# One layer of linear attention with a gated unit: the first tiles' work in another order, operand addresses at multiples of 512 bytes, query steps in smaller pieces

## The chip, the cores and the metric

The kernel runs on one core of one Trainium2 chip. A core has five instruction queues that run beside each other and meet only at semaphores: TensorE (PE in the profile, with PEld for its loads of weights), VectorE (DVE), ScalarE (ACT), GpSimd (POOL) and SyncE (SP), which here issues DMAs alone. Each queue executes its instructions in the order in which they stand in the program. The metric is the device time of one execution in microseconds, lower is better; with several runs the median counts.

## The reference, cut to what matters

The input x has 2048 rows of 512. All of it is float32.

```python
xn = _layernorm(x)
# _A_ref(xn): 32 heads of 16
q, k, v = xn @ wqkv
pq = q @ w_phi;  pk = k @ w_phi                  # per head
phi_q = concat(softmax(pq), softmax(-pq))        # 32 features a head
phi_k = concat(softmax(pk), softmax(-pk))
kv = phi_k^T v;  z = sum over rows of phi_k
s = ((phi_q @ kv) / (phi_q @ z + 1e-6)) @ wo
# _B_ref(xn): 1376 features
g = silu((relu(xn @ W_gate) * (xn @ W_up)) @ W_down)
return x + s * g
```

## The kernel before, in words

**Tiles.** The 2048 rows are 16 tiles of 128. The list `order` takes them in pairs of two blocks, so that tiles 0 and 1, 2 and 3 and so on of the list (this text counts by the list) belong to two blocks that are worked on together. Products run in float32r: each operand is split into a hi part (a copy rounded by ScalarE) and a lo part (the rest, by VectorE or GpSimd), and `mm3` makes three matmuls of one product: lo by hi, hi by lo, hi by hi. Weights for the keys and queries are first multiplied by `w_phi` (`fold`), so that a projection gives pk and pq directly.

**First stage: keys and values.** For each tile n the loop at the end of `layer_kernel` does this: load x; layer norm; transpose on TensorE (`turn`, tile `pxT`), whose result ScalarE copies as the hi part into `XT` and once more as `xf`, and VectorE completes with the lo part (`lo_xt`); project to pk and pv (12 matmuls of 512 columns each); `features`, which turns pk into phi on VectorE and ScalarE (largest and smallest of each head into `mx`, two subtractions into `ek`, two Exp, sum `sm`, reciprocal, product) and splits v into `vhl`; `query`, the projection of an earlier tile to pq, stored to DRAM; `features_split`, which splits phi into hi and lo (`phl`, the lo part on GpSimd) and adds phi to `zacc` with an accumulating DMA; and `kv_products` of tile n-2, which adds phi^T v into four PSUM banks that stay taken (`pkv`). For each odd tile, GpSimd makes four sums and differences of the two tiles of a pair (`sums_x`, tiles `sa` and `sb`), whose hi and lo parts (`sums_hi`, `sums_lo`) also go into `XT`; the second stage uses them.

**Norms.** There are two ways to do a layer norm. `norm_stats`, `norm_scale`, `norm_apply` let ScalarE sum and square and apply (each with a little VectorE, and a power of -0.5 on GpSimd with the constant `mhalf`). `norm_vector` and `norm_vector_apply` do it on VectorE (statistics, aggregate, add, then one two-scalar operation), with the same power on GpSimd. Before the change tiles 0 to 3 go by the second way, all others by the first.

**Before the loop.** The loads of x and of three weights are issued on SyncE; weights arrive while tile 0 is normed. Then, written out by hand: fold and split of the key weights (`wkh`, `wkl`), norm and transpose of tiles 0 and 1, pk of tile 0, hi and lo parts of the value weights (`wv_hi` on ScalarE, `wv_lo` on GpSimd), fold and split of the query weights (`wqh`, `wql`), norms of tiles 2 to 5.

**Second stage: the gated unit.** Eleven blocks of 128 features, in two halves of the rows. `gate_up` computes gate and up for two blocks of rows at once by a scheme of seven products (`pa`, `pb`, `pc`, `pd`) on sums of the operands, of which VectorE reads each result before the next may be added into the same PSUM bank; `down` multiplies with W_down (`py`). Beside it run, in small steps: the preparation of the weights (`f_prep`, sums and splits on GpSimd and ScalarE, stored to DRAM for the second half), and the queries (`q_pair`: fetch and transpose of pq, `bounds`, `shift`, Exp, sums, division, and `q_back`, which multiplies with kv, tile `pnum`). At the end of each half `out_tile` multiplies with wo (`pso`) and combines.

**What sets the order.** All instructions of a queue stay in the order in which the program issues them. A small planner (`Clock`, called `pace`) decides at building time where steps written as generators are put: it keeps an estimate of when each engine is free and each tile ready, and `pump` issues the next step of each generator when its engine's estimated backlog is below a limit. For the preparation of weights that limit is two times the value in `LIMIT` (2,500 ns for GpSimd). A step is what lies between two `yield`s.

**Memory.** Tiles come from pools: `u8`, `u4` and `u2` are slots of 8, 4 and 2 KB a partition; PSUM has eight banks, used in turn (`ps`), so that a new tile waits until the one eight places earlier has been read. In the built program the constants of the compiler take 128 bytes a partition ahead of the first tile. `XT` and all `u8` and `u2` slots start at 128 modulo 512, and the `u4` slots, which come after `ident` (512 bytes) and `mhalf` (128 bytes), at 256 modulo 512. In the matmuls the tiles of value features (`vhl`), of the attention output (`oh`, `ol`) and of transposed phi (`pTh`, `pTl`) come from `u4`; all others come from `XT`, `u8` and `u2`.

Of the kernel before, what the change touches and what calls it, by code (L numbers as in the profile page):

```python
# [13 lines left out]
P = 128  # L14
# [134 lines left out]
def layer_kernel(ctx: ExitStack, tc: tile.TileContext, x, wkT, wqT, wv, wo, wf, cst, out):  # L149
# [12 lines left out]
    def u4(shape, name, dt=F32):  # L162
        return sb.tile(list(shape), dt, tag="u4", bufs=B4, name=name)
# [4 lines left out]
    def small(n, name, bufs=3):  # L168
        return sb.tile([P, n], F32, tag=name, bufs=bufs, name=name)
# [71 lines left out]
        return lambda: split(*map(by_parity, w[k]), even_first(p))  # L241


    XT = sb.tile([P, 8, 2, 2, BT], F32R, tag="XT", name="XT")
    pace.shared = XT.name
    XN, XF, SF = {}, {}, {}
# [128 lines left out]
                PQ[q] = dram((P, 2, 2 * P), f"pq{q[0]}{q[1]}")  # L375
            pace.when(t, lambda q=q, col=col, part=part: nc.sync.dma_start(PQ[q][:, col, :], t[:, part, :]))

    def features(n, pk, pv, between):

        vhl = u4((P, NG, 2, 64), "vhl", F32R)  # L380
        pvg = pv.rearrange("p (g f) -> p g f", g=NG)
        pkv_ = pk.rearrange("p (h f) -> p h f", f=DH)
        sm = small(64, "sm", 2)
        e = u4((P, H, 2, DH), "ek")
        mx = sb.tile([P, 2, H], F32, tag="mx", bufs=2, name="mx")
        nc.vector.tensor_reduce(mx[:, 0, :], pkv_, op=ALU.max, axis=AX.X)
        nc.vector.tensor_reduce(mx[:, 1, :], pkv_, op=ALU.min, axis=AX.X)
        for s in range(2):
            top = mx[:, s, :].unsqueeze(2).to_broadcast([P, H, DH])
            a, b = (top, pkv_) if s else (pkv_, top)  # L390
            nc.vector.tensor_tensor(e[:, :, s, :], a, b, op=ALU.subtract)
            nc.scalar.activation(e[:, :, s, :], e[:, :, s, :], AF.Exp)
            if s == 0:
                nc.scalar.activation(vhl[:, :, 0, :], pvg, AF.Copy)
        between()
        add(nc.vector, vhl[:, :, 1, :], pvg, f32(vhl[:, :, 0, :]), ALU.subtract)
        nc.vector.tensor_reduce(sm, groups(e), op=ALU.add, axis=AX.X)
        nc.vector.reciprocal(pv[:, 0:64], sm)
        VH[n] = vhl
        phi = e if n else zacc  # L400
        nc.vector.tensor_tensor(groups(phi), groups(e), pv[:, 0:64].unsqueeze(2).to_broadcast([P, 64, DH]), op=ALU.mult)
        EK[n] = phi
# [228 lines left out]
    def q_pair(q):  # L631
# [10 lines left out]
        def bounds(j):  # L642
            mx.append(sb.tile([P, 2, H], F32, tag="mx", bufs=2, name="mx"))
            nc.vector.tensor_reduce(mx[j][:, 0, :], pv[j], op=ALU.max, axis=AX.X)
            nc.vector.tensor_reduce(mx[j][:, 1, :], pv[j], op=ALU.min, axis=AX.X)
# [27 lines left out]
        fetch(0)  # L673
        yield "vector", pv[0]
        bounds(0)
        shift(0)
        yield "scalar", es[0]
        expo(0)
# [1 line left out]
        fetch(1)  # L680
        yield "vector", pv[1]
        bounds(1)
        shift(1)
        if q + 1 < NP:
            q_load(q + 1)
# [209 lines left out]
    p = ps((P, P), name="pidle")  # L895
    for _ in range(14):
        nc.tensor.matmul(p, idle, idle, start=True, stop=True)
    mhalf = sb.tile([P, 32], F32, name="mhalf")[:, 0:1]
    nc.vector.memset(mhalf, -0.5)
    zacc = u4((P, H, 2, DH), "zacc")  # L900

# [18 lines left out]
    norm_vector_apply(1)  # L920
    pk = project(0, WK, "pk")
    folds = [fold(WQ, wq_raw[:, k, :], k) for k in range(2)]
    for k in range(KD):
        wv_hi(k)
        if k < 3:
            wv_lo(k)
    folds[0]()
    norm_vector(2)
    folds[1]()
    full_xt(*px)  # L930
    px = turn(1)
    norm_vector_apply(2)
    folds = [fold(WQ, wq_raw[:, k, :], k) for k in range(2, KD)]
    lo_xt(*px)
    wv_lo(3)
    norm_vector(3)
    folds[0]()
    norm_vector_apply(3)
    folds[1]()
    norm_stats(4)  # L940
    norm_scale(4)
    norm_stats(5)

    def all_preps():
        for f in AHEAD:
# [14 lines left out]
    for n in range(N):  # L960
        at[0] = n
        if n + 7 < N:
            load_x(n + 7)
        if n == 2:
            preps = pace.add(all_preps(), 0, 2)
        if n + 4 < N:
            norm_apply(n + 4)
        if n + 5 < N:
            norm_scale(n + 5)
        if n:  # L970
            pk = project(n, WK, "pk")
        if n == 1:
            third = turn(LEAD)
            sums_x(LEAD)
        turned = turn(n + LEAD) if 0 < n < N - LEAD else None
        pace.pump()
        if turned and turned[0] % 2 and n:
            sums_x(turned[0])
        pv = project(n, WV, "pv")
        if n == 0:  # L980
            turned = turn(2)
        pace.pump()

        def between():
            if n == 1:
                lo_xt(*third)
            if turned:
                lo_xt(*turned)
        features(n, pk, pv, between)
        if n >= 1:  # L990
            query(n - 1)
            pace.pump()
            if n % 2 == 0 and n - 1 < N // 2:
                pace.later(4, lambda n=n: spill_x(n - 1))
        if n == 0:
            sums_x(1)
            sums_hi(1)
            sums_lo(1)
        if n + 6 < N:
            norm_stats(n + 6)  # L1000
        if n % 2 and n + 2 < N:
            sums_hi(n + 2)
        features_split(n)
        if n % 2 and n + 2 < N:
            sums_lo(n + 2)
        if n >= 2:
            kv_products(n - 2)
            pace.pump()
# [214 lines left out]
```

## Time and profile before

| | us |
|---|---|
| median of 3 runs | 573.58 (572.75 to 573.88) |
| the profiled execution | 574.12 |
| its span | 572.3 |
| TensorE busy | 563.2 |
| VectorE busy | 411.4 |
| ScalarE busy | 281.4 |
| GpSimd busy | 413.9 |

The profile is of one execution. Its page gives for each engine the time in which it had an instruction running. [...] Rows in order of time give start, duration, engine, line, operation, output and inputs; line 52 is a helper that issues every operation, so tiles tell the operations apart. A matmul of float32 operands has two records, one of float32r has one. The granted clock was 1.00 throughout.

### The profile page before, as it was taken

The numbers are of one execution on the slowest core, as the hardware profiler recorded it, in microseconds if no ns is written. First come the engines' busy times: TensorE is split into PE (matmuls) and PEld (weight loads), VectorE is DVE, ScalarE is ACT, GpSimd is POOL, SyncE is SP. The second block draws the span as 40 slices with busy tenths as digits, with TensorE's granted clock in tenths as the row PEclk, the third lists the DMA queues.
The fourth block names the chain that finished last, engine by engine and source line by source line (L and its number), as shares of the span: only waits on it lengthen the run. The fifth ranks groups of instructions, "written<-read, shape, count | busy, mean of one in ns | idle before, by whom it ended". The sixth has DMA issues, their size and how long they took to land.

```text
span 572.3 us, 8310 instructions
## 1 busy us (share of the span) xinstructions
PE 563.2 (98%) x2688; PEld 470.4 (82%) x2688; DVE 411.4 (72%) x613; ACT 281.4 (49%) x503; POOL 413.9 (72%) x351
## 2 busy tenths in 40 slices
PE   8899999999999999999999999999999999999997
PEld 8787888888888788888888888888888888888886
DVE  4799677676755899699797442599896969874322
ACT  3699687775535436435435142223545544534510
POOL 1569988899867267989986434554669888888476
PEclk9999999999999999999999999999999999999999
DMA  8348999956598918788787999996656766569783
GB/s 292 117 147 216 255 261 276 262 168 184 156 264 261 378 63 293 269 295 273 243 291 254 223 362 417 395 356 243 180 189 208 233 204 195 170 203 312 186 223 144
DMA packets 84682, 138.24 MB, mean 242 GB/s; under 512 B 7840, under 2 KB 34336, under 8 KB 83744
## 3 DMA queue, kind: packets, MB, share of 16 engines
q1 hardware_dynamic: 81184, 125.60, 64.6%
q0 software_dynamic: 3312, 12.06, 11.2%
q8 instruction: 21, 0.34, 0.2%
q14 instruction: 21, 0.17, 0.1%
q10 hardware_dynamic: 144, 0.07, 0.0%
HBM read 77.14 MB, written 52.69 MB: 227 GB/s over the span
## 4 chain that ended last, share of the span: by engine, by line
PE 88%; DVE 5%; POOL 2%; DMA 2%; ACT 1%; issue 1%; SPq 1%; POOLq 0%; DVEq 0%
PE py L52 20%; PE pa L52 10%; PE pc L52 10%; PE pd L52 10%; PE pso L52 8%; PE pq L52 7%; PE pk L52 6%; PE pv L52 6%; PE pb L52 5%; PE pnum L52 3%; PE pkv L52 3%; DMA wvr<-wv 2%; SPq L52 1%; DVE mx L52 1%; PE pxT L52 1%
## 5 line engine op out<-in xcount | busy, mean ns | idle before, releaser
L52 PE MATMUL py<-fdh,hl 128*128 128x512 f32 x176 | 68.5, 389 | 0.0
L52 PE MATMUL py<-fdh,hh 128*128 128x512 f32 x176 | 68.5, 389 | 0.0
L52 PE MATMUL py<-fdl,hh 128*128 128x512 f32 x176 | 68.5, 389 | 0.0
L52 PE MATMUL pa<-XT,wa 128*128 128x512 f32 x264 | 67.6, 390 | 0.0
L52 POOL TENSOR_TENSOR hl<-e,hh 128x512 fp32r<-128x512 f32 x22 | 28.7, 1305 | 42.4 <-ACT hh L52 37.8
L52 PEld LDWEIGHTS pa<-XT,wa 128*128 128x128 f32 x264 | 49.3, 188 | 10.3
L52 ACT ACTIVATE hh<-e 128x512 fp32r<-128x512 f32 x22 | 13.9, 633 | 74.9 <-DVE e L52 65.4
L52 POOL TENSOR_TENSOR phl<-ek,phl 128x1024 fp32r<-128x1024 f32 x15 | 36.1, 2405 | 17.1 <-ACT phl L52 17.1
L52 DVE TENSOR_TENSOR y<-py,y 128x512 f32<-128x512 f32 x40 | 27.5, 688 | 26.8 <-PE py L52 26.6
L52 POOL TENSOR_TENSOR hl<-u,hh 128x512 fp32r<-128x512 f32 x22 | 28.9, 1312 | 23.0 <-ACT hh L52 22.9
L52 PE MATMUL pv<-wvh,XT 128*128 128x512 f32 x128 | 43.5, 401 | 0.0
L52 PE MATMUL pk<-wkh,XT 128*128 128x512 f32 x128 | 42.5, 393 | 0.9 <-DVE ek L52 0.9
L52 PE MATMUL pq<-XT,wqh 128*128 128x512 f32 (+1 forms) x144 | 40.4, 366 | 0.0
L52 PEld LDWEIGHTS py<-fdh,hh 128*128 128x128 f32 x176 | 33.0, 188 | 6.9
L52 PEld LDWEIGHTS py<-fdh,hl 128*128 128x128 f32 x176 | 33.0, 188 | 6.8
L52 PEld LDWEIGHTS py<-fdl,hh 128*128 128x128 f32 x176 | 33.0, 188 | 6.8
L52 POOL TENSOR_TENSOR ez<-eq,zB 128x1024 f32<-128x1024 f32 x16 | 38.5, 2418 | 0.0
L52 PE MATMUL pc<-XT,wc 128*128 128x512 f32 x132 | 35.3, 395 | 0.8 <-DVE e L52 0.8
L52 POOL TENSOR_TENSOR ol<-of,oh 128x1024 fp32r<-128x1024 f32 x8 | 19.2, 2408 | 23.1 <-ACT oh L52 11.2
L52 PE MATMUL pd<-XT,wd 128*128 128x512 f32 x132 | 34.2, 393 | 0.0
L52 PE MATMUL pd<-XT,wc 128*128 128x512 f32 x132 | 33.8, 389 | 0.0
L52 PE MATMUL pc<-XT,wb 128*128 128x512 f32 x132 | 33.7, 389 | 0.0
(154 smaller groups left out, 1598.2 us busy)
## 6 DMA issues: line engine op xcount, KB each, us to landing
zacc<-ek POOLq DMA_DIRECT2D x15, 512.0 KB, 5.4
xts<-XT SPq DMA_DIRECT2D x4, 1792.0 KB, 11.8
XT<-xts SPq DMA_DIRECT2D x7, 1024.0 KB, 17.6
wa<-ws SPq DMA_DIRECT2D x26, 256.0 KB, 3.8
wb<-ws SPq DMA_DIRECT2D x26, 256.0 KB, 5.3
wc<-ws SPq DMA_DIRECT2D x26, 256.0 KB, 5.3
rawg<-wf SPq DMA_DIRECT2D x22, 256.0 KB, 4.4
ws<-wa SPq DMA_DIRECT2D x22, 256.0 KB, 5.6
```

What stands on the lines that cost most here:

```text
L52: return self.tc.keep_in_program_order(op(*a, **k))
```

## The change

- **Addresses.** `mhalf` is made first and with 96 floats instead of 32, so 384 bytes lie between the compiler's 128 and `XT`. `XT` and all `u8`, `u4` and `u2` slots then start at multiples of 512 bytes.
- **`features` in three functions.** `exponents` (maxima, minima and subtractions on VectorE), `exp_part` (one Exp on ScalarE) and the rest. For tile 0, `exponents` is issued right after its pk and the first four parts of the value weights, and both Exp before the loop; for the other tiles the order is as it was.
- **Value weights.** Each lo part follows its hi part; parts 0 and 1 come before the splits of the first two query weights, 2 and 3 after them. All four lo parts are issued before the norms of tiles 2 and 3.
- **Norms.** Tile 4 is normed on VectorE, tile 5 on ScalarE; in the loop, the apply of tile 4 stands at n = 0 and that of tile 5 at n = 1.
- **Sums of tile 1.** `sums_x(1)` and `sums_hi(1)` are issued before the loop, `sums_lo(1)` at n = 1.
- **Transposes.** At n = 0, pk of tile 1 comes before the transpose of tile 2. At n = 1, tile 3 is transposed before pv of tile 1 and tile 4 after it; before, both came ahead of pv.
- **Split of tile 0's phi.** `features_split(0)` moves from the end of n = 0 into n = 1, ahead of the features of tile 1.
- **Preparation of weights.** Its limit goes from two to three.
- **Query steps.** In `q_pair` a `yield` stands between `bounds` and `shift`, for both halves, so that the planner may issue other work between them.

```diff
@@ -241,6 +241,7 @@
         return lambda: split(*map(by_parity, w[k]), even_first(p))
 
 
+    mhalf = sb.tile([P, 96], F32, name="mhalf")[:, 0:1]
     XT = sb.tile([P, 8, 2, 2, BT], F32R, tag="XT", name="XT")
     pace.shared = XT.name
     XN, XF, SF = {}, {}, {}
@@ -375,12 +376,9 @@
                 PQ[q] = dram((P, 2, 2 * P), f"pq{q[0]}{q[1]}")
             pace.when(t, lambda q=q, col=col, part=part: nc.sync.dma_start(PQ[q][:, col, :], t[:, part, :]))
 
-    def features(n, pk, pv, between):
-
-        vhl = u4((P, NG, 2, 64), "vhl", F32R)
-        pvg = pv.rearrange("p (g f) -> p g f", g=NG)
+    def exponents(pk):
+
         pkv_ = pk.rearrange("p (h f) -> p h f", f=DH)
-        sm = small(64, "sm", 2)
         e = u4((P, H, 2, DH), "ek")
         mx = sb.tile([P, 2, H], F32, tag="mx", bufs=2, name="mx")
         nc.vector.tensor_reduce(mx[:, 0, :], pkv_, op=ALU.max, axis=AX.X)
@@ -389,9 +387,21 @@
             top = mx[:, s, :].unsqueeze(2).to_broadcast([P, H, DH])
             a, b = (top, pkv_) if s else (pkv_, top)
             nc.vector.tensor_tensor(e[:, :, s, :], a, b, op=ALU.subtract)
-            nc.scalar.activation(e[:, :, s, :], e[:, :, s, :], AF.Exp)
-            if s == 0:
-                nc.scalar.activation(vhl[:, :, 0, :], pvg, AF.Copy)
+        return e
+
+    def exp_part(e, s):
+        nc.scalar.activation(e[:, :, s, :], e[:, :, s, :], AF.Exp)
+
+    def features(n, e, raised, pv, between):
+
+        vhl = u4((P, NG, 2, 64), "vhl", F32R)
+        pvg = pv.rearrange("p (g f) -> p g f", g=NG)
+        sm = small(64, "sm", 2)
+        if not raised:
+            exp_part(e, 0)
+        nc.scalar.activation(vhl[:, :, 0, :], pvg, AF.Copy)
+        if not raised:
+            exp_part(e, 1)
         between()
         add(nc.vector, vhl[:, :, 1, :], pvg, f32(vhl[:, :, 0, :]), ALU.subtract)
         nc.vector.tensor_reduce(sm, groups(e), op=ALU.add, axis=AX.X)
@@ -673,6 +683,7 @@
         fetch(0)
         yield "vector", pv[0]
         bounds(0)
+        yield "vector", pv[0]
         shift(0)
         yield "scalar", es[0]
         expo(0)
@@ -680,6 +691,7 @@
         fetch(1)
         yield "vector", pv[1]
         bounds(1)
+        yield "vector", pv[1]
         shift(1)
         if q + 1 < NP:
             q_load(q + 1)
@@ -895,7 +907,6 @@
     p = ps((P, P), name="pidle")
     for _ in range(14):
         nc.tensor.matmul(p, idle, idle, start=True, stop=True)
-    mhalf = sb.tile([P, 32], F32, name="mhalf")[:, 0:1]
     nc.vector.memset(mhalf, -0.5)
     zacc = u4((P, H, 2, DH), "zacc")
 
@@ -920,26 +931,31 @@
     norm_vector_apply(1)
     pk = project(0, WK, "pk")
     folds = [fold(WQ, wq_raw[:, k, :], k) for k in range(2)]
-    for k in range(KD):
+    for k in range(2):
         wv_hi(k)
-        if k < 3:
-            wv_lo(k)
+        wv_lo(k)
+    early = exponents(pk)
     folds[0]()
+    folds[1]()
+    for k in range(2, KD):
+        wv_hi(k)
+        wv_lo(k)
     norm_vector(2)
-    folds[1]()
     full_xt(*px)
     px = turn(1)
+    lo_xt(*px)
+    folds = [fold(WQ, wq_raw[:, k, :], k) for k in range(2, KD)]
+    for s in range(2):
+        exp_part(early, s)
+    norm_vector(3)
     norm_vector_apply(2)
-    folds = [fold(WQ, wq_raw[:, k, :], k) for k in range(2, KD)]
-    lo_xt(*px)
-    wv_lo(3)
-    norm_vector(3)
+    sums_x(1)
     folds[0]()
+    folds[1]()
     norm_vector_apply(3)
-    folds[1]()
-    norm_stats(4)
-    norm_scale(4)
     norm_stats(5)
+    norm_vector(4)
+    sums_hi(1)
 
     def all_preps():
         for f in AHEAD:
@@ -962,45 +978,49 @@
         if n + 7 < N:
             load_x(n + 7)
         if n == 2:
-            preps = pace.add(all_preps(), 0, 2)
-        if n + 4 < N:
+            preps = pace.add(all_preps(), 0, 3)
+        if n == 0:
+            norm_vector_apply(4)
+        elif n + 4 < N and n > 1:
             norm_apply(n + 4)
         if n + 5 < N:
             norm_scale(n + 5)
-        if n:
+
+        now, late = {0: ((), ()), 1: ((3,), (4,))}.get(n, ((n + LEAD,) if n < N - LEAD else (), ()))
+        if n > 1:
             pk = project(n, WK, "pk")
-        if n == 1:
-            third = turn(LEAD)
-            sums_x(LEAD)
-        turned = turn(n + LEAD) if 0 < n < N - LEAD else None
+        turned = [turn(m) for m in now]
         pace.pump()
-        if turned and turned[0] % 2 and n:
-            sums_x(turned[0])
+        for m in now:
+            if m % 2:
+                sums_x(m)
         pv = project(n, WV, "pv")
         if n == 0:
-            turned = turn(2)
+            pk = project(1, WK, "pk")
+            turned = [turn(2)]
+        turned += [turn(m) for m in late]
+        if n == 1:
+            norm_apply(5)
+            features_split(0)
+            sums_lo(1)
         pace.pump()
 
         def between():
-            if n == 1:
-                lo_xt(*third)
-            if turned:
-                lo_xt(*turned)
-        features(n, pk, pv, between)
+            for t in turned:
+                lo_xt(*t)
+        e, early = early or exponents(pk), None
+        features(n, e, n == 0, pv, between)
         if n >= 1:
             query(n - 1)
             pace.pump()
             if n % 2 == 0 and n - 1 < N // 2:
                 pace.later(4, lambda n=n: spill_x(n - 1))
-        if n == 0:
-            sums_x(1)
-            sums_hi(1)
-            sums_lo(1)
         if n + 6 < N:
             norm_stats(n + 6)
         if n % 2 and n + 2 < N:
             sums_hi(n + 2)
-        features_split(n)
+        if n:
+            features_split(n)
         if n % 2 and n + 2 < N:
             sums_lo(n + 2)
         if n >= 2:
```

## The prediction

> **What bounds the kernel now.** I read the page's first lines, then the list of what TensorE waited for, then the rows in order of time around each wait.
>
> ```profile
> span 572.3 us, 8310 instructions
> PE 563.2 (98%) x2688; PEld 470.4 (82%) x2688; DVE 411.4 (72%) x613; ACT 281.4 (49%) x503; POOL 413.9 (72%) x351
> PE 88%; DVE 5%; POOL 2%; DMA 2%; ACT 1%; issue 1%; SPq 1%; POOLq 0%; DVEq 0%
> ```
>
> TensorE is busy for 563.2 of 572.3 us and holds 88% of the chain. The change takes no matrix product away, so time can come from only two places: the 9.1 us in which PE is idle, and the spacing of the 2688 matmul records. The profiled execution took 574.12 us, 1.8 us more than its span; the runs' median is 573.58, 0.54 below it. I work out differences on the trace and take them from 573.58.
>
> ```profile
> PE pxT L52 <- ACT xn L52: 1.2, 1, 1.2
> PE pk L52 <- DVE ek L52: 0.9, 1, 0.9
> PE pv L52 <- POOL wvl L52: 0.8, 1, 0.8
> PE pc L52 <- DVE e L52: 0.8, 1, 0.8
> ```
>
> Four waits of 3.7 us in all (columns: sum, times, longest). The first three lie in the first 44 us, where the change reorders work; the fourth is in the query steps, which the change cuts up. So each part of the edit does face a wait. But a wait that goes may only uncover the next one, so I walk through both places.
>
> **The head, up to the third tile.** Rows of the trace in order of time (start, duration, engine, output<-inputs; in brackets the idle time before):
>
> ```profile
> 13.54 1.51 DVE L52 TENSOR_SCALAR xn<-xt,bm,br 128x512 f32<-128x512 f32 x1
> 15.96 1.15 ACT L52 ACTIVATE wvh<-wvr 128x512 fp32r<-128x512 f32 x2 [2.26 <-DMA wvr<-wv]
> 17.63 0.69 DVE L52 TENSOR_TENSOR wql<-pfold,wqh 128x512 fp32r<-128x512 f32 x1 [2.58 <-ACT wqh L52]
> 18.02 0.48 PE L52 MATMUL pv<-wvh,XT 128*128 128x512 f32 x1
> 19.99 1.29 POOL L52 TENSOR_TENSOR wvl<-wvr,wvh 128x512 fp32r<-128x512 f32 x1
> 21.34 0.50 PE L52 MATMUL pv<-wvl,XT 128*128 128x512 f32 x1 [0.78 <-POOL wvl L52]
> 22.08 0.68 DVE L52 BATCH_NORM_STATS2 bs<-xt 128x6 f32<-128x512 f32 x1
> 23.90 0.55 DVE L52 TENSOR_SCALAR xn<-xt,bm,br 128x512 f32<-128x512 f32 x1
> 25.10 0.60 PE L52 MATMUL pxT<-ident,xn 128*128 128x128 f32 x4
> 25.96 1.28 DVE L52 TENSOR_REDUCE mx<-pk 128x32 f32<-128x512 f32 x2
> 26.89 0.65 PE L52 MATMUL pxT<-ident,xn 128*128 128x128 f32 x4 [1.19 <-ACT xn L52]
> 27.16 0.68 DVE L52 TENSOR_TENSOR ek<-pk,mx 128x512 f32<-128x512 f32 x1
> 28.86 0.74 POOL L52 TENSOR_TENSOR sb<-xf,sa 128x256 f32<-128x256 f32 x1
> 29.02 0.69 DVE L52 TENSOR_TENSOR vhl<-pv,vhl 128x512 fp32r<-128x512 f32 x1
> 43.03 0.68 DVE L52 TENSOR_TENSOR ek<-mx,pk 128x512 f32<-128x512 f32 x1
> 43.86 0.47 PE L52 MATMUL pk<-wkh,XT 128*128 128x512 f32 x1 [0.92 <-DVE ek L52]
> 50.75 0.68 DVE L52 TENSOR_TENSOR ek<-mx,pk 128x512 f32<-128x512 f32 x1
> 53.56 0.39 PE L52 MATMUL pk<-wkh,XT 128*128 128x512 f32 x1
> ```
>
> *Parts of the weights.* Now the last lo part of wv waits on POOL behind a norm's pow and ends at 21.28, 0.06 before PE resumes. The change issues all four lo parts before that norm. Their hi parts need the DMA, which lets ScalarE start at 15.96. ScalarE now first does the two wqh parts (before, they came after wvh), so wvh 2 and 3 end at about 17.65 instead of 17.1. POOL then does two lo parts of 1.29 each from 17.15 and ends at about 19.75. PE begins pv at 18.02 and comes to the last lo part, its eleventh matmul, some 2.4 us later (0.3 for the first, then 0.23 each), at 20.4. The wait of 0.8 goes, with 0.1 of restart.
>
> *Exponents of tile 0.* Two reductions and two subtractions (25.96 to 28.4: about 2.4 us) move to 15.05, where DVE sat idle for 2.58 us. Their cover is that idle time. They end at 17.5, and wql starts where it did. The two Exp of tile 0 also go to an earlier place on ScalarE; nothing of PE waits there.
>
> *Norms.* Tile 4's norm moves from ScalarE (two passes, accumulators, an apply) to DVE: statistics (0.68 at 22.08 for tile 3), two small operations and an apply (0.55 at 23.90). The apply is dear when POOL is working: the row at 13.54 has the same operation at 1.51. [...] That price is at stake for tile 3, because the sums of tile 1 (four POOL pieces of about 0.74, here the last is at 28.86) now run at about 22.0 to 24.9. So tile 3's apply ends between 24.0 and 25.4. Its transpose is wanted at about 23.95 (pv until 20.75, pk's twelve matmuls until 23.5, then tile 2's transpose) and waits 0.2 to 1.5 us instead of the 1.2 for tile 4 now. Tile 4's transpose comes after a whole pv and doesn't wait.
>
> *What is late next.* Those two gains are not simply the answer, for the next wait is DVE's. The third tile's pk takes a PSUM bank that is free only after the subtractions of tile 2 (43.03 + 0.68). From vhl at 29.02 to the end of these DVE is busy but for about 1.0 us. In the new order vhl's turn comes at about 27.75. Its hi part on ScalarE now stands behind the hi copies of the sums (new place), which wait for the last POOL piece at 24.9; then come two copies of a tile's transpose and vhl itself, 0.5 each, up to 27.0; then DVE does tile 2's lo part. From there the same 14.7 us of work, less up to 1.0 of idle time, ends at 41.5 to 42.5. PE itself would be there at 40.9 plus the small wait above. So pk starts at 41.6 to 42.6 instead of 43.86: 1.3 to 2.3 us off. I take 1.8, the middle. All three head waits together are worth that and not the 2.9 they add up to. One tile later DVE's subtraction ends at 51.43 and PE comes at 53.56: 2.1 us in hand, so nothing is given back there.
>
> *More preps.* Limit 2 becomes 3, so weights for the gate stage enter the queues of POOL and ScalarE sooner and stand ahead of the split of phl. A phl is used two tiles later:
>
> ```profile
> 42.31 2.38 POOL L52 TENSOR_TENSOR phl<-ek,phl 128x1024 fp32r<-128x1024 f32 x1 [2.59 <-ACT phl L52]
> 52.60 1.13 PE L52 MATMUL pkv<-phl,vhl 128*128 128x256 f32 x8
> ```
>
> It ends at 44.7 and is wanted at 52.6, so 7.9 us cover what is put before it (a 128x512 POOL piece is 1.29). Its price is nothing; without that cover two pieces, 2.6 us. SP's stores of prepared weights and loads of x move with it; no PE row waits for them here, and I cost them at nothing.
>
> **The query steps.** A yield between bounds and shift lets other DVE work in.
>
> ```profile
> 186.21 1.29 DVE L52 TENSOR_REDUCE mx<-pq 128x32 f32<-128x512 f32 x2
> 188.01 0.68 DVE L52 TENSOR_TENSOR eq<-mx,pq 128x512 f32<-128x512 f32 x1
> 189.60 1.52 PE L52 MATMUL pd<-XT,wc 128*128 128x512 f32 x6
> 190.53 0.72 DVE L52 STREAM_TRANSPOSE pq<-pql 128x512 f32<-128x512 f32 x1
> 191.15 0.67 DVE L52 TENSOR_TENSOR e<-pc,u 128x512 f32<-128x512 f32 x1
> 191.88 1.67 PE L52 MATMUL pc<-XT,wc 128*128 128x512 f32 x6 [0.76 <-DVE e L52]
> ```
>
> PE adds to pc only after DVE has read it. It would come there at 190.96 (six matmuls from 189.60) and starts at 191.88. In the new program the first reduction is followed by two of the gate stage's DVE operations instead of the subtractions, and the read of pc stands before the second transpose, not behind it: it ends 0.6 to 0.7 sooner, at 191.2. Of 0.92 about 0.25 is left: 0.7 off, with 0 (another operation takes the place) and 0.9 as bounds. The later query steps hold up no PE row now and cost nothing: the same instructions in another order beside a busy PE.
>
> **The addresses.** mhalf's tile of 384 bytes before XT, instead of 128 behind the identity, moves XT, the 8 KB and 2 KB tiles from 128 to 0 modulo 512 and the 4 KB tiles from 256 to 0. It adds no instruction. What it may do is seen where the two operands of a matmul now differ:
>
> ```profile
> 30.49 0.28 PE L52 MATMUL pq<-XT,wql 128*128 128x256 f32 x1
> 32.65 0.28 PE L52 MATMUL pq<-XT,wql 128*128 128x256 f32 x1
> 200.74 0.39 PE L52 MATMUL py<-fdl,hh 128*128 128x512 f32 x1
> 201.65 0.39 PE L52 MATMUL py<-fdh,hh 128*128 128x512 f32 x1
> 545.13 0.40 PE L52 MATMUL pso<-woh,ol 128*128 128x512 f32 x1
> 547.92 0.39 PE L52 MATMUL pso<-woh,ol 128*128 128x512 f32 x1
> ```
>
> py has weights and moving rows both at 128: its two rows are four matmuls apart, 227 ns each. pso has its weights in 4 KB tiles (256) and its moving rows at 128: twelve apart, 232 ns each. If the addresses cause that, all pairs at 0 agree as py's do, and pso's 180 matmuls of 512 columns gain 5 ns: 0.9 us. No row has a pair at 0, so the bounds come from both sides. The two pq rows are 18 matmuls of 256 columns apart, 120 ns each; 256 columns more cost 107 ns, so 512 alone are 214 and 13 ns are a floor under every matmul. At best that floor goes (13 ns better), at worst all pairs do as pso does (5 ns worse). I take py's value, since every pair that now agrees modulo 512 has it.
>
> Sum: 1.8 + 0.7 + 0.9 = 3.4 off 573.58, forecast **570.2 us** (0.6%).
>
> **Rivals.**
> *(a) The floor falls.* The 13 ns come from operands that straddle 512-byte blocks, and go: 2512 matmuls (2184 of 512 columns, 328 of 256) by 13 ns are 32.7 us, with the 2.5 of the reordering about 538. For it: the floor is the same at both sizes, as if it came with the 512 bytes of weights. Against: nothing shows that addresses cause it. [...]
>
> *(b) The other side: residue 0 doesn't settle.* Then the 2004 other matmuls of 512 columns are spaced as pso's are, 5 ns more: 10.0, against 2.5 off: 581.1. It decides from 1.3 ns per matmul on. For it: pso shows that an address alone may cost this much. Against: there the operands differ, here they agree.
>
> *(c) POOL holds PE up.* Tile 3's apply is blocked more than once, or preps push phl past its 7.9 us, and the planner's new order repeats it at a later tile: two pieces of 1.29 at each of two places, 5.2, less 3.4: 575.4. For it: the apply at 13.54. Against: phl's slack.
>
> *(d) It doesn't do what it says.* DVE's chain holds pk at 43.8 as now, e still comes late, pso stays at 232: 573.6.
>
> **How the numbers follow.** Forecast 0.57, (a) 0.11, (b) 0.09, (c) 0.12, (d) 0.11. A change under 0.2% (1.15 us) can't be told from none. Faster: the forecast and (a), 0.68; same: (d), 0.11; slower: (b) and (c), 0.21. The likeliest case's own range is 568.7 (the waits wholly gone, 2.9 + 0.9 and restarts of 0.2, and pso's 0.9) to 572.3 (the head's lower bound alone). The range of 8 in 10 takes in (c) and (d) and, below, a floor that falls by a quarter, 3 ns on 2184 matmuls, 6.6 more off: 563.5 to 575.5. It leaves out (b) and the full (a).
>
> **What would show it.** Right: the last wv lo ends near 19.8 and pv runs through; the third tile's pk starts near 42; the waits for xn, wvl and e in the list of waits are under 0.3 or gone; pso's rows 227 ns apart. Wrong: py's rows more than 1 ns off 227 (addresses decide all); pk at 43.8 (DVE's chain was not shortened); a new wait of PE for phl.

## The result, and the profile after

The changed kernel takes 569.81 us (median of 20 runs, 567.54 to 575.55), the kernel before on the same chip 573.75 (20 runs, 572.75 to 574.99). The ratio is 0.9937, with a 95% interval of 0.9917 to 0.9957: 0.6% faster. 570.2 was forecast. The spread is new: the kernel before stays within 2.3 us, the changed one covers 8, and four of its 20 runs lie above 573.

The profiled execution of the changed kernel happens to be the longest of all, 575.55 us. Two lines of its page (the busy times, and the share of each engine in the chain that ended last):

```profile
PE 562.5 (98%) x2688; PEld 472.0 (82%) x2688; DVE 410.3 (72%) x615; ACT 280.3 (49%) x498; POOL 413.3 (72%) x351
PE 82%; DMA 6%; DVE 4%; issue 3%; POOL 3%; ACT 1%; SPq 0%; POOLq 0%; ACTq 0%; DVEq 0%
```

DMA has risen from 2% to 6% of the chain. What TensorE waited for in it (sum, times, longest), in a span of 573.7 us:

```profile
PE pv L52 <- ACT pqs L52: 3.2, 1, 3.2
...
PE pk L52 <- DVE ek L52: 0.8, 1, 0.8
PE pso L52 <- POOL ol L52: 0.4, 1, 0.4
```

The waits for xn, wvl and e of the profile before are gone. A wait of 3.2 us that was not there stands at the head of the list. The same kernel was profiled a second time, in an execution of 570.48 us, 5.1 shorter, with a span of 568.7 us:

```profile
PE pk L52 <- DVE ek L52: 1.6, 2, 0.8
...
PE pso L52 <- POOL ol L52: 0.4, 1, 0.4
```

Here the wait of pv for pqs is missing, though DMA still has 4% of this chain, so the rise by itself is not that wait. This is the execution to compare with the profile before. Its first 42 us, in order of time (start, duration, engine, output and inputs, idle time before):

```profile
16.66 0.67 DVE L52 TENSOR_TENSOR ek<-mx,pk 128x512 f32<-128x512 f32 x1
17.17 2.55 POOL L52 TENSOR_TENSOR wvl<-wvr,wvh 128x512 fp32r<-128x512 f32 x2 [1.09 <-ACT wvh L52]
17.26 1.27 DVE L52 TENSOR_TENSOR wql<-pfold,wqh 128x512 fp32r<-128x512 f32 x2
17.92 0.48 PE L52 MATMUL pv<-wvh,XT 128*128 128x512 f32 x1
22.74 0.99 DVE L52 TENSOR_SCALAR xn<-xt,bm,br 128x512 f32<-128x512 f32 x1
23.48 1.03 PE L52 MATMUL pxT<-ident,xn 128*128 128x128 f32 x8
27.41 0.68 DVE L52 TENSOR_TENSOR vhl<-pv,vhl 128x512 fp32r<-128x512 f32 x1
40.32 0.68 DVE L52 TENSOR_TENSOR ek<-mx,pk 128x512 f32<-128x512 f32 x1
41.14 0.47 PE L52 MATMUL pk<-wkh,XT 128*128 128x512 f32 x1 [0.79 <-DVE ek L52]
```

PE begins pv 0.1 us earlier than before (17.92 against 18.02), and the pk that the prediction calls the third tile's 2.7 us earlier (41.14 against 43.86). By the list's numbers, which start at 0, it is tile 3's. The weights' lo parts end at 19.72, tile 3's apply at 23.73, and the two transposes run as one group of eight with nothing between.

Matmuls of the output projection in the profiled execution of 575.55 us, twelve apart as in the prediction:

```profile
545.53 0.39 PE L52 MATMUL pso<-woh,ol 128*128 128x512 f32 x1
548.25 0.39 PE L52 MATMUL pso<-woh,ol 128*128 128x512 f32 x1
```

The records, 0.39 us each, overlap, so the distance from one start to the next is taken as the cost of a matmul. 2.72 us over 12 are 227 ns, where it was 232.

The new wait, in the same execution, first SyncE's queue, then ScalarE, then TensorE:

```profile
79.61 0.52 SPq L52 DMA_DIRECT2D xts<-XT  x1
81.31 6.24 SPq L52 DMA_DIRECT2D xt<-x  x1
87.64 1.53 SPq L52 DMA_DIRECT2D pq<-pqs  x2
89.34 1.35 SPq L52 DMA_DIRECT2D rawg<-wf  x2
```
```profile
95.39 0.42 ACT L52 ACTIVATE wa<-rawg 128x256 fp32r<-128x256 f32 x1 [7.29 <-DMA rawg<-wf]
96.01 0.42 ACT L52 ACTIVATE wa<-rawg 128x256 fp32r<-128x256 f32 x1 [0.20 <-DMA rawg<-wf]
96.33 0.58 ACT L52 ACTIVATE pqs<-pq 128x512 f32<-128x512 f32 x1
```
```profile
96.96 0.50 PE L52 MATMUL pv<-wvh,XT 128*128 128x512 f32 x1 [3.16 <-ACT pqs L52]
...
100.29 0.63 PE L52 MATMUL pv<-wvl,XT 128*128 128x512 f32 x1
100.71 0.63 PE L52 MATMUL pv<-wvh,XT 128*128 128x512 f32 x1
101.14 0.63 PE L52 MATMUL pq<-XT,wql 128*128 128x512 f32 x1
```

The granted clock of TensorE around that place (stretch, its length, PE busy and its instructions, granted clock, then DMA):

```profile
97.00:98.30 1.30, 1.30 (x6) 1.00 0.89 332
98.40:101.70 3.30, 3.30 (x9) 0.50 0.12 40
101.80:103.00 1.20, 1.20 (x6) 1.00 0.00 0
```

Read it backwards. pv needs the PSUM bank that pqs empties. pqs stands on ScalarE behind wa, the rounded copy of a weight that is being prepared for the second stage. wa waits 7.29 us for its load. That load was issued at 89.34, because the issue of a load of x in front of it on SyncE lasted 6.24 us; and that one followed the store xts of 1,792 KB. For 1.3 us after the wait matmuls go at full clock; then for 3.4 us the granted clock is 0.50 and they are 0.43 us apart (100.29, 100.71, 101.14) instead of 0.23, which is 1.7 us more. In the execution of 570.48 us the same instructions read:

```profile
77.59 0.52 SPq L52 DMA_DIRECT2D xts<-XT  x1
80.44 2.26 SPq L52 DMA_DIRECT2D xt<-x  x1
...
85.53 1.69 SPq L52 DMA_DIRECT2D rawg<-wf  x2
```
```profile
91.13 0.71 ACT L52 ACTIVATE wa<-rawg 128x256 fp32r<-128x256 f32 x2
91.75 0.58 ACT L52 ACTIVATE pqs<-pq 128x512 f32<-128x512 f32 x1
```

The load is issued 3.8 us earlier and ScalarE doesn't wait for it. Of these 3.8 us 1.15 are no delay of the queue: the longer execution is late by that much from its first pv on (19.07 against 17.92), with everything behind it.

### The profile page after: what moved, and what is told of

Same layout as the page of the kernel before. It is cut to its first block, busy times and chain, and to the rows that moved or that the text cites. A ratio compares the mean times of both kernels' runs of the same rounds, so it can differ in the third digit from the quotient of the medians.

```text
span 573.7 us, 8321 instructions
## 1 busy us (share of the span) xinstructions
PE 562.5 (98%) x2688; PEld 472.0 (82%) x2688; DVE 410.3 (72%) x615; ACT 280.3 (49%) x498; POOL 413.3 (72%) x351
## 4 chain that ended last, share of the span: by engine, by line
PE 82%; DMA 6%; DVE 4%; issue 3%; POOL 3%; ACT 1%; SPq 0%; POOLq 0%; ACTq 0%; DVEq 0%
PE py L52 18%; PE pc L52 10%; PE pa L52 10%; PE pd L52 10%; PE pq L52 7%; PE pv L52 7%; PE pk L52 6%; PE pb L52 5%; PE pso L52 4%; PE pnum L52 2%; PE pkv L52 2%; DMA sx<-x 2%; DMA of<-ol 1%; DMA woh<-wo 1%; DMA rawg<-wf 1%
## 5 line engine op out<-in xcount | busy, mean ns | idle before, releaser
L52 POOL TENSOR_TENSOR y<-y,ys 128x512 f32<-128x512 f32 x24 | 31.1, 1298 | 5.0 <-ACT ys L52 4.9
```

What stands on the lines that cost most here:

```text
L52: return self.tc.keep_in_program_order(op(*a, **k))
```

## The experiments

Differences below are those of the median to the median of the kernel before on the same chip (574.10, 574.04 and 574.00 us in the three groups), the changed kernel itself being 3.94 below it both times that it was measured. The ratios come with their 95% intervals from all the runs; they needn't be the quotient of the two medians.

### Addresses alone

The kernel before, with the diff's two lines for `mhalf` and nothing else.

```diff
+    mhalf = sb.tile([P, 96], F32, name="mhalf")[:, 0:1]
     XT = sb.tile([P, 8, 2, 2, BT], F32R, tag="XT", name="XT")
...
-    mhalf = sb.tile([P, 32], F32, name="mhalf")[:, 0:1]
```

> The kernel before with the new addresses alone (mhalf of 96 floats ahead of XT). Theory of the prediction (pairs that agree modulo 512 settle at 227 ns): pso's 180 matmuls go from 232 to 227 ns, 0.9 us faster, so 572.8. Rival (addresses do nothing): 573.7 and pso at 232. Second rival (matmuls settle sooner everywhere after a change of their kind): up to 2.5 us faster, 571.2, with fewer intervals between 228 and 236 ns in pk, pv and pkv.

Measured: 572.35 us (6 runs), 1.75 less, ratio 0.9975 (0.9961 to 0.9990). pso's spacing is 227 ns. Adding up over both traces how much each pair of like matmuls lies above 226.7 ns (512 columns), 120 (256) or 111 (128), with waits left out, gives about 2.35 us before and 1.0 here: 1.3 less, of which pso's rows are 1.0. The remaining 0.4 of the 1.75 can't be assigned within the interval. Traces can't assign it either, because the wait of 0.8 us for wvl, absent from this trace, varies between executions whose first tiles have the same order: it is 0.5, 0.5 and 0.2 us in three other runs below and absent in the one with all addresses at 256. Of the DMAs, the store xts changed too (last column: time from issue to landing, which the traces have for one of the four stores, in both rows the third), first before, then here:

```profile
xts<-XT SPq DMA_DIRECT2D x4, 1792.0 KB, 11.8
```
```profile
xts<-XT SPq DMA_DIRECT2D x4, 1792.0 KB, 7.2
```

The prediction had asked of the addresses only what they do to matmuls. Here the third store lands 4.6 us sooner, but that isn't the addresses alone: in a run below that has them too, the changed kernel without the yields, the third store takes 11.4. What goes with the addresses in every trace is smaller. The packets of the first store end 8.0 to 8.3 us after its issue in the six traces with the old addresses (8.2 in the kernel before), where XT starts at 128 modulo 512, and 6.7 to 7.1 us after it in the eight with the new ones (6.7 in the changed kernel). Why the start of XT matters to the store isn't shown.

### All addresses at 256 modulo 512

The same, with 32 floats instead of 96, so that all large tiles start at 256 modulo 512.

```diff
+    mhalf = sb.tile([P, 32], F32, name="mhalf")[:, 0:1]
     XT = sb.tile([P, 8, 2, 2, BT], F32R, tag="XT", name="XT")
...
-    mhalf = sb.tile([P, 32], F32, name="mhalf")[:, 0:1]
```

> The kernel before with mhalf's tile of 128 bytes made ahead of XT: XT and all large slots start at 256 modulo 512, so every pair of operands agrees modulo 512 and none is at a multiple of 512. Theory (agreement counts, not the multiple): pso's rows 227 ns apart and py's still 227; the time as with addresses at 0, 572.4 on the chip where before takes 574.1, a ratio of 0.997 to 0.999. Rival (operands must start at multiples of 512): pso's rows stay at 232 or all rows go there, 574 to 584.

Measured: 572.60 us (12 runs), 1.44 less, ratio 0.9977 (0.9966 to 0.9987). Spacing above the base is about 1.0 us in all, xts lands after 7.2 us. Both are as with addresses at 0. So for 227 ns it is enough that the two operands agree modulo 512; a multiple of 512 isn't needed, and for the store 256 is as good as 0. The only difference that any run has is 128 bytes, so agreement modulo 256 would explain the rows as well.

### The two yields alone

```diff
         bounds(0)
+        yield "vector", pv[0]
         shift(0)
...
         bounds(1)
+        yield "vector", pv[1]
         shift(1)
```

> The kernel before with the two yields of the query steps alone. Theory: PE's wait for e near 191 us falls from 0.9 to about 0.25, 0.7 us faster: 573.0. Rival (another operation takes the place): the wait stays at 0.7 or more, 573.7. Second rival: it goes wholly and later query steps bring waits of their own: slower than 574.

Measured: 573.25 us (12 runs), 0.85 less, ratio 0.9988 (0.9974 to 1.0003). In its trace the wait of pc for e is 0.4 us instead of 0.8. More goes elsewhere: the kernel before has delays of 0.1 to 0.25 us in TensorE's rows of the query steps (at 195, 218, 251, 440 and 456 us), and here they are gone. All delays of this kind between 186 and 460 us, pc's included, come to 2.4 us before and 1.1 here. The median's 0.85 is near the prediction's 0.7, but the wait that the prediction named is only 0.4 of it; the interval just includes no gain.

### The new order of the first tiles alone

The changed kernel with the old addresses, without the yields and with the limit at two.

```diff
-    mhalf = sb.tile([P, 96], F32, name="mhalf")[:, 0:1]
...
-        yield "vector", pv[0]
...
-        yield "vector", pv[1]
...
+    mhalf = sb.tile([P, 32], F32, name="mhalf")[:, 0:1]
...
-            preps = pace.add(all_preps(), 0, 3)
+            preps = pace.add(all_preps(), 0, 2)
```

> The changed kernel with the old addresses, without the two added yields and with the limit at two: the new order of the first five tiles alone. Theory: 1.8 us off before by the prediction, a ratio of 0.997; the third tile's pk starts at 42 to 42.6 and the waits for xn and wvl are gone. Rival (the new order shifts the planner's clock so that weights prepared on GpSimd are late for stage two, as with the limit at two in the changed kernel): pk as above, but a wait of PE for weights of about 1.5 us between 170 and 195 us and a ratio of 1.000 or above.

Measured: 577.90 us (6 runs), 3.86 **more** than before, ratio 1.0055 (1.0037 to 1.0074). tile 3's pk starts at 41.21, so the head does all that it should. The loss is 130 us later (what TensorE waited for):

```profile
PE pc L52 <- DVE e L52: 3.3, 1, 3.3
PE pb L52 <- POOL wb L52: 1.4, 1, 1.4
```

pb is the second stage's second product, and wb the lo part of its weights on GpSimd. The row of that operation here, in the kernel before, and in the changed kernel's execution of 570.48 us:

```profile
170.14 1.55 POOL L52 TENSOR_TENSOR wb<-tab,wb 128x512 fp32r<-128x512 f32 x1
```
```profile
157.35 1.58 POOL L52 TENSOR_TENSOR wb<-tab,wb 128x512 fp32r<-128x512 f32 x1
```
```profile
155.51 1.59 POOL L52 TENSOR_TENSOR wb<-tab,wb 128x512 fp32r<-128x512 f32 x1
```

The planner places the preparation of weights by its own estimate of time, and the new order shifts that estimate. With a limit of two it puts this operation behind a split of phl two tiles later, 13 us late. The larger wait, of pc for e, stands behind another order on VectorE: a whole step of the query (188.64 to 191.79) lies between the reads of pa and of pb there, and in the kernel before it lay ahead of both. And after that wait the granted clock is 0.50 for 3.4 us, 1.7 us more. The rival of the expectation is right, though wb is the smaller part.

### The limit of three alone

The kernel before, with one digit changed.

```diff
-            preps = pace.add(all_preps(), 0, 2)
+            preps = pace.add(all_preps(), 0, 3)
```

> The kernel before with the limit at three and nothing else. Theory of the prediction (the limit costs and gives nothing in the old order, where weights were in time with two as well): a ratio of 0.998 to 1.002, no wait of PE for weights or for pqs. Rival (earlier weights take a wait away, as they did in the changed kernel, 4 us): 0.993. Second rival (the copies of weights stand ahead of their load as in the changed kernel): above 1.003, with a wait of pv for pqs.

Measured: 579.94 us (4 runs), 5.94 more, ratio 1.0105 (1.0092 to 1.0118). The theory of the prediction falls. The places, in order: SyncE, the chain, ScalarE, TensorE.

```profile
86.90 7.73 SPq L52 DMA_DIRECT2D xt<-x  x1
94.76 2.53 SPq L52 DMA_DIRECT2D pq<-pqs  x2
```
```profile
95.87 5.75 DMA pq<-pqs
```
```profile
101.73 0.63 ACT L52 ACTIVATE xn<-xt 128x512 f32<-128x512 f32 x1 [4.07 <-DMA pq<-pqs]
```
```profile
106.02 0.76 PE L52 MATMUL pk<-wkh,XT 128*128 128x512 f32 x1 [3.60 <-DVE ek L52]
```

More weights prepared means more stores ahead of the store xts on SyncE. xts was issued at 76.81 in the kernel before and at 85.57 here, and the load of x behind it occupied the queue for 7.73 us instead of 1.10. The small store of pqs stood behind that, ScalarE waited, by the profile, until it had landed, DVE's chain followed, and PE lost 3.6 us and 1.7 more by 3.4 us at a granted clock of 0.50.

### The changed kernel with the limit at two

```diff
-            preps = pace.add(all_preps(), 0, 3)
+            preps = pace.add(all_preps(), 0, 2)
```

> The changed kernel with the limit of the preparation of weights back at two; all else of the change stays. In the profiled execution of the changed kernel PE stood 3.2 us at 97 us, because ScalarE's copy of weights (wa) stands ahead of the copy of pq (pqs) that frees a PSUM bank, and waits for its load; the twelve matmuls after that ran at about half speed, 2 us more. Theory of the prediction (the limit costs nothing, the stall is an accident of DMA): the median stays within 1 us of the changed kernel's 569.8, and its executions spread as widely (567.5 to 575.5). Rival (the limit puts wa ahead of pqs, and that is the cause of the spread): no wait of PE for pqs, the median near 567.7, all executions within 1.5 us.

Measured: 573.84 us (12 runs), no change from before, ratio 1.0001 (0.9984 to 1.0019). The limit isn't neutral, as the theory had it, and taking it back isn't a gain, as the rival had it, but a loss of 3.7 us. The list has pc waiting 2.0 us for e and pb 1.4 for wb, the same two as with the new order alone (and, in the profiled execution, the longest, pso 2.8 for ol near the end). So in the old order the limit of three costs 5.9 us, and in the new one it gives 3.7.

### The changed kernel with the old addresses

```diff
-    mhalf = sb.tile([P, 96], F32, name="mhalf")[:, 0:1]
...
+    mhalf = sb.tile([P, 32], F32, name="mhalf")[:, 0:1]
```

> The changed kernel without the new addresses: mhalf is 32 floats and stands where it stood; the order of all instructions is that of the changed kernel. Theory: the addresses give 0.9 us, so 570.7, with pso back at 232 ns. Rival (addresses do nothing): 569.8.

Measured: 579.01 us (6 runs, 578.14 to 580.82), 4.91 more than before, ratio 1.0092 (1.0076 to 1.0109). Against the changed kernel that is 8.9 us, five times what the addresses give alone. The list of waits begins

```profile
PE pv L52 <- ACT pqs L52: 4.6, 1, 4.6
PE pk L52 <- DVE ek L52: 2.2, 2, 1.4
```

and the load of rawg is issued at 90.45. What only some executions of the changed kernel show, these show at its full size: the mean granted clock is 0.992 to 0.994 in all six, and in the trace it is 0.50 for 6.8 us.

### The weight's copy put later

The changed kernel; the planner is told that the load of the second block prepared ahead lands 2.5 us later, so its preparation, wa first, stands some tiles later on ScalarE and GpSimd.

```diff
         nc.sync.dma_start(RAW[f][1], wf[f][:, 1024:])
+        if f in AHEAD[1:]:
+            for t in (*RAW[f][0], RAW[f][1]):
+                pace.ready[t.name] = pace.ready.get(t.name, pace.now) + 2500
```

> The changed kernel, with one thing different: the planner believes that the load of the second block that is prepared ahead lands 2.5 us later, so the copies of its first weights (wa) stand some tiles later on ScalarE and no longer right ahead of the copy pqs. Theory (the 3.3 us wait of pv at 96.96, and the half-speed matmuls behind it, are ScalarE waiting for that load): the wait is gone, the slow executions of 573 to 575 us go, the median comes to 568.3 (567.5 to 569) and the spread within 567.5 to 570. Rival (the executions differ for another reason, and the wait is only in the one that was profiled): median 569.8, some executions still above 573. Second rival (a later block of weights is late for stage two, as with the limit at two): above 571, with a wait of PE for weights between 170 and 195 us.

Measured: 568.74 us (5 runs, 567.18 to 571.11), 5.30 less than before, ratio 0.9896 (0.9880 to 0.9912). This interval doesn't meet the changed kernel's (0.9917 to 0.9957), so by the intervals this version beats both, though on five runs, which overlap with those of the changed kernel. Its waits, in its longest execution:

```profile
PE pfold L52 <- DMA wkT<-wkT: 1.1, 2, 0.9
...
PE pk L52 <- DVE ek L52: 0.8, 1, 0.8
PE pso L52 <- POOL ol L52: 0.7, 1, 0.7
```

No wait for pqs, and no run above 571.2. The upper end was forecast at 570 and is 571.1; this execution waits for the landing of the first weights and, near the end, for ol.

### The same with the old addresses

The edit of the last run on top of the changed kernel with the old addresses.

> The kernel of the run above with the old addresses (mhalf behind the identity). Theory (of the 9 us that the addresses were worth in the changed kernel, all but about 1.7 came from the wait for the load, which the old addresses made later): 570.0, between 569 and 571.5, with pso's rows 232 ns apart and no wait of pv for pqs. Rival (the addresses speed up something else in the new order): 576 or more.

Measured: 569.68 us (4 runs, 569.48 to 570.60), 4.36 less than before, ratio 0.9924 (0.9910 to 0.9937); no wait for pqs; pso's rows 232 ns apart. So with the load out of the way the addresses are worth 0.9 us, and the remaining 8 of their 8.9 go with the place of that load and of what waits for it. The edit moves the whole preparation of that block, not wa alone, so the runs show this for the preparation and not for the one copy.

### The same without the yields

The version with wa later, without the two yields.

> The kernel with wa later (568.7 before), without the two yields in the query steps. Theory of the prediction (the first query step holds up the read of pc by one transpose): the wait for e at about 190 us is back with 0.7 to 0.9 us and the time is 569.4 to 569.7. Rival (in the new order a whole step of the query, transpose, bounds and shift, stands ahead of the read of pc, as in the run of the head alone, where that wait was 3.3): 571 to 572.5, with a wait of 2 us or more. Second rival: the limit alone has put other work there, nothing changes, 568.7.

Measured: 569.45 us (5 runs), 4.55 less than before and 0.75 more than with the yields, though the two intervals overlap (ratio 0.9919, 0.9906 to 0.9932, here). The six matmuls of pd and the next pc:

```profile
187.73 1.52 PE L52 MATMUL pd<-XT,wc 128*128 128x512 f32 x6
189.24 1.65 PE L52 MATMUL pc<-XT,wc 128*128 128x512 f32 x6
```

1.51 us apart, where six matmuls take 1.36: a stall of 0.15 and not the 0.9 that was expected. In the new order DVE comes to this point earlier anyway: its read of pc ends 1.5 us after pd's start, against 2.2 in the kernel before. The rest of the 0.75 may lie in several delays of 0.1 to 0.25 us in the query steps (at 192, 216 and 437 us), which are absent with the yields: all delays between 186 and 460 us come to 1.7 us here and 0.4 with them.

### The same with the old order of the first tiles

The version with wa later, with the new addresses, the yields and the limit of three, but with the order of the first tiles, before and in the loop, that the kernel before has.

> The kernel with wa later, with the first five tiles in the old order (addresses, yields and the limit of three stay). Theory (the head is worth 1.6 to 1.8 us, as pk of the third tile shows): 570.3 to 570.6, with the waits for xn and wvl back and pk at about 43.5. Rival (the head only uncovers later waits and is worth nothing at the end): 568.7. Second rival (the old order moves the planner's clock, so that weights are late for stage two or ScalarE waits for a load): above 571.5 with a new wait between 90 and 195 us.

Measured: 579.06 us (6 runs), 10.4 more than with the new order, ratio 1.0087 (1.0066 to 1.0107). The list of waits begins with pk for ek, 5.7 us in three places, at 105 and 118 us among them. There the chain runs through stores of prepared weights and the accumulating DMA of phi, 9.11 us long. The third store xts is issued at 86.17, as late as with the limit of three alone (85.57) and not as in the changed kernel (79.61 and 77.59). So the order of the first five tiles decides, through the planner, whether the limit of three puts more into SyncE's queue ahead of that store.

### The changed kernel once more

No edit.

> The changed kernel itself once more, beside the next three. Theory (its executions differ by whether the load of the second block lands before ScalarE comes to wa): a median near 569.8, and in whichever execution is profiled the time and the wait go together: with no wait of pv for pqs it lies at 567 to 570, with one above 572. Rival: an execution above 572 without that wait, or one below 570 with it.

Measured: 570.06 us (12 runs, 568.10 to 575.61), ratio 0.9937 (0.9918 to 0.9957). The profiled execution, 570.48 us, has no wait for pqs; it is a little over the 570 that the theory gave for that case, since pk waits once more for ek at 90.3 us (0.8, behind DVE's wait for the accumulating DMA). With 575.55 there are two profiled executions, one of each kind. The others show their kind by their mean granted clock, which 3.4 us at half clock lower by 0.003. Of the first 20 executions the four above 573 have 0.996 and all others 0.998 to 1.000; of these 12 the one at 575.61 has 0.993 and the others 0.998 to 1.000; in the 14 executions of the three versions with wa later and the new order it is never under 0.998. The number doesn't say where the clock fell. The 16 shorter ones of the first 20 have a median of 569.05, so the four raise it by 0.8 us.

## Why the prediction was right, and where it wasn't

The total was met within 0.4 us, and the mechanisms at TensorE are those of the text. But the sum holds a term of nothing that isn't nothing, so part of the agreement is luck.

**Parts of the weights.** Last lo part at 19.75 forecast, 19.72 found; pv runs through. Right.

**Exponents of tile 0.** End 17.5 forecast, 17.33 found; wql follows at 17.26. Hidden, as said.

**Norms.** The apply of tile 3 ends at 23.73, forecast 24.0 to 25.4: it is lengthened to 0.99 us and not to 1.51. In the profile before, the apply of 1.51 runs beside two of GpSimd's operations of 128x512, and no row of GpSimd stands beside that of 0.55 (23.90):

```profile
13.47 2.71 POOL L52 TENSOR_TENSOR wvl<-wvr,wvh 128x512 fp32r<-128x512 f32 x2
```

In the execution of 570.48 us tile 3's apply runs beside the sums of tile 1, of 128x256:

```profile
22.71 0.74 POOL L52 TENSOR_TENSOR sb<-xf 128x256 f32<-128x256 f32 x1
23.41 0.91 POOL L52 TENSOR_TENSOR sa<-sa,xf 128x256 f32<-128x256 f32 x1
```

How the one lengthens the other isn't shown. The wait of 0.2 to 1.5 us for its transpose doesn't exist. This term was mis-sized.

**What is late next.** DVE's subtraction holds pk, as the text said, and 0.79 us of that wait are left. From the start of pv to that pk pass 23.22 us instead of 25.84: 2.6, forecast 1.8 (1.3 to 2.3). Part of the difference is that tile 3 lost nothing and vhl came at 27.41, not 27.75. The rest is the profile before. In the six traces with the old order that stretch takes 24.85 to 25.84 us, longest in the one that the prediction read, while the eight with the new order agree within 0.03 us. The gain is 1.6 to 2.6, and 1.8 lies in it.

**Query steps.** Forecast 0.7, with 0.25 of the wait left. In the changed kernel nothing is left:

```profile
192.87 1.52 PE L52 MATMUL pd<-XT,wc 128*128 128x512 f32 x6
194.23 1.52 PE L52 MATMUL pc<-XT,wc 128*128 128x512 f32 x6
```

1.36 us, six matmuls. But with the new order most of that is due to the order: without the yields 0.15 would be left. The size of 0.75 and 0.85 in the two comparisons of medians fits, the reason only in part. The sentence that the later query steps "hold up no PE row now and cost nothing" is wrong: their delays of 0.1 to 0.25 us come to about 1.0 us in the kernel before and go with the yields.

**Addresses.** Forecast 0.9 by pso's 5 ns; that came (1.0). Other matmuls gave some 0.3 more, and the store xts got faster, of which the text said nothing. Rivals (a) and (b) fall: pq's matmuls of 256 columns are still 120 ns apart and py's of 512 still 227, so the floor that the text worked out from these two didn't move, and no kind of matmul of 512 columns became slower.

**More preps.** This step failed: "Its price is nothing", and "SP's stores of prepared weights and loads of x move with it; no PE row waits for them here, and I cost them at nothing." It looked at phl on GpSimd, which was indeed covered, and dismissed the queue that was not. Alone the limit costs 5.9 us, through SyncE. In the changed kernel it gives 3.7, since it repairs a delay that the text had not seen either: the new order moves the planner's clock, and with the old limit the weights of stage two come 13 us later. And in some executions it takes back 5 us by the wait for a load.

The parts alone add up to 3.9 + 5.9 - 1.75 - 0.85 = 7.2 us more than before; together they give 3.9 less. So the account of the result is another one than the sum of 3.4. From the profile before to that of 570.48 us the sum closes. The change gains 2.6 in the head, 2.0 in the query steps (0.9 of it at pc) and 1.3 in spacing. It gives back 0.9 where pk waits at 90 us behind the accumulating DMA, 0.7 at pso's wait for ol (0.4 of idle time; the rest is in the spacing around it: in the execution of 575.55 us, with the same wait, pso starts 0.80 us after the matmul ahead of it and the next one 0.33 after that, where two steps take 0.45) and 0.7 behind the last matmul. What is left is 3.6, the difference of the spans. The version with wa later is 5.3 below before, so the changed kernel gives back 1.4 at the median: 0.8 of it are the four executions with the half clock, and where the rest goes isn't shown. Single executions lie up to 7 us above that version's median. Rival (c) named the right kind of cost, preparation of weights that holds PE up, but on GpSimd's phl, not on SyncE, and not as a matter of single executions.

**Left open.** What decides in one execution how long the load of x behind the large store occupies SyncE (2.26 or 6.24 us) wasn't varied by itself; the two executions differ also in when xts was issued, by 2.0 us, of which 1.15 are the later start of the whole.

## What to carry to other kernels

An order written out by hand that feeds a planner isn't local: moving work in the first 40 us moved weights by 13 us at 157, and each part of the change, alone, had to be seen with the planner's answer to it. When a step puts more work into a queue, follow that queue to the end, the DMA queue of SyncE above all: here the small store of pqs behind a load's issue of 7.73 us cost TensorE a wait of 3.6 us, and the load of rawg behind one of 6.24 us a wait of 3.2. And when a kernel's runs spread more after a change than before, look in a long and a short execution for an engine that waits for a DMA in front of something urgent; here putting that instruction, and the preparation that it belongs to, later was worth another 1.4 us at the median.

## What the runs showed of the hardware

- The spacing of these float32r matmuls of 512 columns goes with where the two operands start, relative to each other: 227 ns when both agree modulo 512 (128 in py's rows before, 256 and 0 here), 232 when they are 128 apart (pso before). At 256 columns pkv, whose operands were 128 apart too, went only from 120.4 to 119.1 ns.
- After 3.16 us without a matmul TensorE went on at full clock for 1.3 us, and then its granted clock was 0.50 for 3.4 us, with 0.43 us per matmul of 512 columns, so the wait of 3.2 us cost about 4.9. Waits of 2.45 us (the old order of the first tiles, at 118 us) and 2.8 us (the limit at two, at 564 us) were followed by the half clock as well, while one of 2.37 us (the old order, at 106 us) was not. What sets off the half clock isn't shown. It lasted 3.4 us or, behind the wait of 4.6 us, twice that.
- The issue behind a store of 1,792 KB on SyncE lasted up to 7.8 us, and the next issues waited with it; the store's own issue takes 0.5 to 0.6 in most cases, and the median issue of the queue 0.4. In all 14 traces, with four such stores each, the issue that follows ends 4.85 to 9.4 us after the store's began, so one that starts at once is a long one. Why it ends no sooner isn't shown.
